# Where TensorE's two operands start in a partition: every pair of the second mixture 64 bytes apart modulo 512, and all tiles on multiples of 64 bytes

## The chip, the cores and the metric

One core of one Trainium2 chip runs the whole program in one launch. The metric is device time in microseconds (us), the median of several executions; lower is better. A core has five engines with queues of their own: TensorE (PE; its weight loads are listed apart as PEld), VectorE (DVE), ScalarE (ACT), GpSimd (POOL) and SyncE (SP, which only issues DMAs here). Tiles stand in SBUF, a memory of 128 partitions; a tile takes the same bytes of every partition, and "address" means here the byte at which it starts in each partition.

## The reference, cut to what matters

Three parts follow one another. The second mixture, to which the change belongs, takes most of the time.

```python
x = attention(q, k, v, M_prev, z_prev, beta)      # 2304 rows of 512
x = soft_mixture(x, phi, w1, w2)                   # 32 slots, 8 experts
# second mixture, N=2304 rows, D=512, E=8 experts, F=1024
P = exp(x @ w_gate - max)
for _ in range(8):
    P /= P.sum(1, keepdims=True) + 1e-09
    P /= P.sum(0, keepdims=True) + 1e-09
    P *= N / E
for e in range(E):
    h = np.maximum(x @ w1[e], 0.0)
    out += P[:, e:e+1] * (h @ w2[e])
```

## The kernel before, in words

The kernel first does the attention (to about 273 us), then the soft mixture (to about 327 us), then the second mixture. In the second mixture the work is cut into 72 units: 8 experts `e` by 9 groups `u` of 256 rows. Each unit is one `layer1` (8 matmuls of 256 columns, line 1035, which gives `x @ w1[e]` for 256 rows) and the product with `w2[e]`.

For the first six units (`RAW = 6`) the second product is made plainly, by `plain` (line 1321), with matmuls of 512 columns. For the other 66 it is made from seven half-size products in the manner of Strassen, in the order `ORDER = ("p5", "p1", "p7", "p6", "p2", "p3", "p4")`. A product (`product`, lines 1344 to 1357) is twelve matmuls of 256 columns: four steps `f`, and in each step three matmuls, since both factors are split into a high and a low part:

```python
for f in range(KH):
    nc.tensor.matmul(o_, hh[:, f, :], wh[:, f, :], start=f == 0, stop=False)
    nc.tensor.matmul(o_, hh[:, f, :], wl[:, f, :], start=False, stop=False)
    nc.tensor.matmul(o_, hl[:, f, :], wh[:, f, :], start=False, stop=f == KH - 1)
```

The first operand (`hh`, `hl`: tiles `a11`, `a12`, `a22`, `s1` to `s4`, each with `h` or `l` behind its name) is the stationary one, which a weight load (PEld) brings into the array: 128 numbers, 512 bytes, per partition. The second (`wh`, `wl`: tiles `T1`, `T2`, `T4`, and `BB1`, `BB2`, which hold the other quarters of `w2`) is the moving one: 256 numbers, 1024 bytes. In a row of the profile `y<-BB1h,s3h` the moving operand stands first and the stationary one second. `layer1` has `a4` (named `a` in the rows) as its stationary and `c4T` as its moving operand. The step `f` moves an operand on by 512, 1024 or 2048 bytes, so that it changes no address modulo 512.

The order of the work on TensorE, VectorE, ScalarE and GpSimd is written out by hand. TensorE goes through unit `g` as p5, p1, `layer1` of unit `g + 1`, p7, p6, p2, p3, p4, with some small matmuls put between (in four of an expert's nine units four transposes, line 1221, stand between p7 and p6; in one, `prepare_a`, line 992). The results of `layer1` are turned into the fourteen stationary tiles by VectorE, ScalarE and GpSimd (`hidden`, lines 1055 to 1076), and `collect` (line 1370) adds the products into `accA`, `accB` and `accD` on VectorE. `layer1` of the next unit may start once VectorE has written `a22l` (line 1072), which is the last to read its two PSUM buffers.

Tiles belong to pools, and pools stand one behind the other from the front of a partition; each tile takes its size rounded up to a multiple of 32 bytes. `T1` and `T2` of even experts and `BB1` are in pool `mA`, the stationary tiles in `mB`, `T4`, `T1` and `T2` of odd experts and `BB2` in `mC`, `a4` in `mD`. `cst` is the pool at the front of the program, with the tile `sacc`.

Of the kernel before, what the change touches and what calls it, by code (L numbers as in the profile page):

```python
# [8 lines left out]
F32 = mybir.dt.float32  # L9
BF16 = mybir.dt.bfloat16  # L10
F32R = mybir.dt.float32r
# [10 lines left out]
def infini_attention_soft_moe_sinkhorn_moe(  # L22
# [18 lines left out]
    E = moe2_w1.shape[0]  # L41
    FF = moe2_w1.shape[1] * moe2_w1.shape[4]
    NS = moe_phi.shape[2]
    SPE = NS // E
    P = 128
# [8 lines left out]
    NTT = N // P  # L54
# [14 lines left out]
    cst = ctx.enter_context(tc.tile_pool(name="cst", bufs=1))  # L69
# [16 lines left out]
        nc.vector.tensor_add(stk, stk, ident[:, 32 * j : 32 * j + 32])  # L86
    soT = cst.tile([P, KD, NS], F32, name="soT")
    wg_sb = cst.tile([P, KD, E], F32, name="wg_sb")
    sacc = cst.tile([P, 1], F32, name="sacc")
    mrow = [cst.tile([1, NS], F32, name=f"mrow{b}") for b in range(B)]  # L90


# [668 lines left out]
    with bctx:  # L761
# [57 lines left out]
        for g in range(E // 4):  # L819
# [3 lines left out]
            for n in range(FF // 512):  # L823
# [3 lines left out]
                for c in range(KD):  # L827
                    for j in range(4):
                        e = SPE * (4 * g + j)
# [41 lines left out]

    mA = ctx.enter_context(tc.tile_pool(name="mA", bufs=1, reuse_waits="tile"))
    mB = ctx.enter_context(tc.tile_pool(name="mB", bufs=1, reuse_waits="tile"))
    mC = ctx.enter_context(tc.tile_pool(name="mC", bufs=1, reuse_waits="tile"))
    mD = ctx.enter_context(tc.tile_pool(name="mD", bufs=1, reuse_waits="tile"))
    ps_l = ctx.enter_context(tc.tile_pool(name="ps_l", bufs=1, space=PSUM, reuse_waits="tile"))
# [91 lines left out]
        )  # L968


    sel = mD.tile([P, 4, 160], F32R, name="sel")
    nc.vector.tensor_scalar(
        out=sel.rearrange("p j c -> p (j c)"), in0=ones[:, 0:1].to_broadcast([P, 640]),
# [2 lines left out]
    for r in (0, 2, 4):  # L976
# [1 line left out]
        nc.vector.tensor_copy(  # L978
            sel[:, :, 32 * r : 32 * r + 32], ident.rearrange("p (j s) -> p j s", j=4)
        )  # L980
    a2s, a4s, G = {}, {}, {}

    def aux(nm):
        return ps_a.tile([P, 512], F32, tag="a", name=nm)
# [13 lines left out]
    def split_a(e):  # L998
        pa = a2s[e]
        ahi = mB.tile([P, 256], F32R, tag="ahi", name="ahi")  # L1000
        nc.scalar.activation(out=ahi, in_=pa[:, 0:256], func=AF.Copy)
        alo = mB.tile([P, 256], F32R, tag="alo", name="alo")
        nc.vector.tensor_tensor(
            out=alo, in0=pa[:, 0:256], in1=ahi.bitcast(F32), op=ALU.subtract
        )
        a2s[e] = ahi, alo
        a4s[e] = mD.tile([P, FF], F32R, tag="a4", name="a4", bufs=2)

    def spread_a(e, n):

# [97 lines left out]

    soR = soT.rearrange("p c (o s) -> p c o s", o=1)
    Pr = mB.tile([P, NTT, E], F32, name="Pr")  # L1110
    Cw = mD.tile([P, NTT, NS], F32, name="Cw")

    gsel = mD.tile([P, E + NS], F32R, name="gsel")
    m1 = mD.tile([P, 1], F32, name="m1")
    m2 = mD.tile([1, 1], F32, name="m2")

    def gate_slots():
        soB = G["soB"] = mB.tile([P, KD, 4, NS], F32, tag="c4", name="soB")
# [51 lines left out]
        nc.scalar.activation(out=Pr, in_=Pr, func=AF.Exp, bias=m1)  # L1170

    def balance_rows():
        rr = mB.tile([P, NTT], F32, tag="rr", name="rr")
        nc.vector.tensor_reduce(out=rr, in_=Pr, op=ALU.add, axis=AX.X)
        nc.vector.tensor_scalar_add(rr, rr, 1e-9)
        nc.vector.reciprocal(rr, rr)
        nc.vector.tensor_tensor(
            out=Pr, in0=Pr, in1=rr.rearrange("p (t o) -> p t o", o=1).to_broadcast([P, NTT, E]),
            op=ALU.mult,
        )  # L1180
        cs = G["cs"] = mB.tile([P, E], F32, tag="cs", name="cs")
        nc.vector.tensor_reduce(
            out=cs, in_=Pr.rearrange("p t e -> p e t"), op=ALU.add, axis=AX.X
        )
# [56 lines left out]
    for n in range(8):  # L1241
        beside(9 + 3 * n, balance_rows)
        beside(10 + 3 * n, sum_columns)
        beside(11 + 3 * n, balance_columns)
# [43 lines left out]
    for e in range(1, E):  # L1288
        v = NU * (e - 1)
        for i in range(5):  # L1290
            c_steps(v + 6 + i, e, 2 * i, min(2 * i + 2, NU))
        at(v, 0, load_w1, e, e % 2)
        at(v + 3 * (e == 1), 4, load_raw, e)
        at(v + 1, 3, prepare_a, e)
        at(v + 1, 4, split_a, e)
        for n in range(2):
            at(v + 1, 5 + 2 * n, spread_a, e, n)
            at(v + 1, 6 + 2 * n, store_a, e, n)
        for i in range(2):
            for n, nm in enumerate(("T1", "T2", "T4")):  # L1300

                s = 29 + 4 * (3 * i + n) if e == 1 else 7 * (v + 2 + 3 * i + n) + 1
                beside(s, w_sum, e, nm, i, "P")
                beside(s + 2 - (e == 1), w_hi, e, nm, i)
                beside(s + 3 - (e == 1), w_lo, e, nm, i, "P")
            at(v + 6 + i, 2, w_sum, e, "T3", i, "P")
        for nm, k in (("B11", 2), ("T3", 4), ("B21", 6), ("B22", 8)):
            for i in range(2):
                at(v + 8, k + i, w_hi, e, nm, i)
                at(v + 8, k + i + (nm[0] == "B" and nm[1] == "2"), w_lo, e, nm, i, "D" if nm == "B22" and i else "P")  # L1310
# [99 lines left out]
    with tc.manual_schedule(engines={E_.PE, E_.DVE, E_.Activation, E_.Pool}):  # L1410
# [4 lines left out]
        prepare_a(0)  # L1415
        gate_slots()
        split_a(0)
        spread_a(0, 0)
        spread_a(0, 1)
# [105 lines left out]
```

## Time and profile before

| | |
|---|---|
| time, median of 3 runs | 1181.48 us |
| lowest and highest | 1179.54 and 1184.17 us |
| the profiled execution's own time | 1182.51 us |
| its span, first to last instruction | 1180.7 us |
| mean granted TensorE clock | 0.986 |
| TensorE busy | 1120.1 us, 95% |
| VectorE, ScalarE, GpSimd busy | 865.7, 656.3, 641.8 us |
| chain that ended last, by engine | PE 75%, DVE 11%, ACT 7%, DMA 3%, issue 2%, POOL 1% |

All terms of a sum are in the time of the profiled execution, whose span is 1.81 us shorter than its own time and whose own time is 1.03 us above the median. The start of a row in a timeline is in us from the span's start. A matmul of this program lasts about 280 ns by its row, but the next one starts long before it ends: what TensorE needs for one more matmul is the distance from start to start.

### The profile page before, as it was taken

How to read it: one execution, taken by the hardware profiler on the slowest of the kernel's cores; microseconds unless marked ns; L12 is line 12 of the kernel's file. 1: busy time of each engine (PE TensorE's matmuls, PEld its weight loads, DVE VectorE, ACT ScalarE, POOL GpSimd, SP SyncE). 2: the span in 40 equal slices, each digit the busy share in tenths (PEclk: the TensorE clock that was granted, in tenths of full speed). 3: DMA queues.
4: the chain of work that ended last, by engine and by line, in shares of the span. 5: the costliest groups of instructions: out<-in, count | busy, mean ns of one | idle time of the engine just before them, and what ended most of it. 6: DMA issues, size and time to landing. Idle time of an engine off the chain costs nothing.

```text
span 1180.7 us, 24363 instructions
## 1 busy us (share of the span) xinstructions
PE 1120.1 (95%) x9247; PEld 1018.6 (86%) x9247; DVE 865.7 (73%) x1891; ACT 656.3 (56%) x1422; POOL 641.8 (54%) x585
## 2 busy tenths in 40 slices
PE   6899999979799999999999999999999999999998
PEld 4677777764287888999999999999999999999998
DVE  6888888874337566677778767777876777788886
ACT  6788888741233487546545644654564465456342
POOL 5433323200323297577677767767776776686443
PEclk9999999998989999999999999999999999999999
DMA  6677686249702004002100400210040031000111
GB/s 158 192 200 226 197 245 178 74 187 376 309 6 71 1 2 143 1 2 82 62 2 1 143 2 1 92 53 1 1 143 1 2 108 37 2 1 19 42 50 54
DMA packets 37412, 102.32 MB, mean 87 GB/s; under 512 B 6448, under 2 KB 13232, under 8 KB 33200
## 3 DMA queue, kind: packets, MB, share of 16 engines
q1 hardware_dynamic: 36864, 100.69, 26.5%
q8 instruction: 73, 1.20, 0.4%
q14 instruction: 43, 0.35, 0.1%
q10 hardware_dynamic: 432, 0.09, 0.0%
HBM read 96.04 MB, written 4.72 MB: 85 GB/s over the span
## 4 chain that ended last, share of the span: by engine, by line
PE 75%; DVE 11%; ACT 7%; DMA 3%; issue 2%; POOL 1%; SPq 0%; ACTq 0%; DVEq 0%; POOLq 0%
PE y L1356 16%; PE y L1354 16%; PE y L1355 16%; PE l L1035 6%; PE y L1321 5%; PE po L436 3%; PE pt L399 2%; ACT sm L360 2%; DMA wm<-in_moe_w_dram 1%; PE pa L992 1%; DVE sm L356 1%; PE pc L1221 1%; PE ph L830 1%; DVE f L1059 1%; DMA raw<-in_moe_w_dram 1%
## 5 line engine op out<-in xcount | busy, mean ns | idle before, releaser
L1059 DVE SCALAR_TENSOR_TENSOR f<-l,f 128x512 f32<-128x512 f32 x264 | 181.4, 687 | 56.6 <-ACT a11h L1065 44.4
L1076 POOL TENSOR_TENSOR s1l<-f,s1h 128x512 fp32r<-128x512 f32 x66 | 88.4, 1340 | 170.0 <-ACT s1h L1065 165.9
L1370 DVE TENSOR_TENSOR accA<-accA,y 128x512 f32<-128x512 f32 (+1 forms) x129 | 86.6, 671 | 57.1 <-PE y L1356 51.6
L1065 ACT ACTIVATE a12h<-l 128x512 fp32r<-128x512 f32 x72 | 43.1, 598 | 121.6 <-DVE f L1059 121.6
L1076 POOL TENSOR_TENSOR s4l<-f,s4h 128x512 fp32r<-128x512 f32 x66 | 86.0, 1303 | 39.9 <-ACT s4h L1065 39.8
L1370 DVE TENSOR_TENSOR accB<-accB,y 128x512 f32<-128x512 f32 x129 | 88.3, 684 | 13.7 <-PE y L1356 2.3
L1035 PE MATMUL l<-c4T,a 128*128 128x256 f32 x576 | 82.7, 286 | 9.2 <-DVE a22l L1072 8.3
L1076 POOL TENSOR_TENSOR s2l<-f,s2h 128x512 fp32r<-128x512 f32 x66 | 85.9, 1301 | 0.8 <-ACT s2h L1065 0.8
L1076 POOL TENSOR_TENSOR s3l<-f,s3h 128x512 fp32r<-128x512 f32 x66 | 86.0, 1303 | 0.3 <-ACT s3h L1065 0.3
L1035 PEld LDWEIGHTS l<-c4T,a 128*128 128x128 f32 x576 | 75.0, 190 | 12.4 <-DVE a22l L1072 10.8
L360 ACT ACTIVATE sm<-sm,mn 128x128 f32<-128x128 f32 (+3 forms) x128 | 71.1, 556 | 19.5 <-DVE mn L356 17.9
L965 POOL TENSOR_TENSOR BB1l<-raw,BB1h 128x512 fp32r<-128x512 f32 x32 | 41.0, 1293 | 68.9 <-ACT BB1h L959 68.9
L1354 PE MATMUL y<-T2h,s2h 128*128 128x256 f32 x264 | 76.9, 291 | 0.0
L1354 PE MATMUL y<-BB2h,a12h 128*128 128x256 f32 x264 | 75.0, 284 | 0.0
L1355 PE MATMUL y<-BB2l,s4h 128*128 128x256 f32 x264 | 74.6, 283 | 0.1
L1354 PE MATMUL y<-BB1h,a11h 128*128 128x256 f32 x264 | 73.4, 278 | 1.3 <-DVE accB L1370 1.3
L1356 PE MATMUL y<-T4h,a22l 128*128 128x256 f32 x264 | 74.6, 283 | 0.0
L1356 PE MATMUL y<-BB2h,a12l 128*128 128x256 f32 x264 | 74.5, 282 | 0.0
L1356 PE MATMUL y<-BB2h,s4l 128*128 128x256 f32 x264 | 74.5, 282 | 0.0
L1354 PE MATMUL y<-BB2h,s4h 128*128 128x256 f32 x264 | 74.5, 282 | 0.0
L1354 PE MATMUL y<-T4h,a22h 128*128 128x256 f32 x264 | 74.3, 281 | 0.0
L1356 PE MATMUL y<-T1h,s1l 128*128 128x256 f32 x264 | 74.1, 281 | 0.0
(313 smaller groups left out, 4219.0 us busy)
## 6 DMA issues: line engine op xcount, KB each, us to landing
wm<-in_moe_w_dram SPq DMA_DIRECT2D x32, 1024.0 KB, 7.7
w<-in_moe_w_dram SPq DMA_DIRECT2D x32, 512.0 KB, 4.4
raw<-in_moe_w_dram SPq DMA_DIRECT2D x32, 512.0 KB, 4.1
qd<-in_q_dram SPq DMA_DIRECT2D x30, 288.0 KB, 4.2
kd<-in_k_dram SPq DMA_DIRECT2D x30, 288.0 KB, 4.5
qp<-in_q_dram SPq DMA_DIRECT2D x16, 288.0 KB, 3.4
vt<-in_v_dram SPq DMA_DIRECT2D x16, 256.0 KB, 2.7
out_dram<-accB SPq DMA_DIRECT2D x18, 128.0 KB, 1.8
```

Source lines behind the costliest of these rows:

```text
L360: nc.scalar.activation(out=sm[:, 0:n], in_=sm[:, 0:n], func=AF.Exp, scale=-1.0, bias=mnc, accum_out=X.sums[:, i, h : h + 1],)
L436: nc.tensor.matmul(po[64 * h : 64 * h + 64, c0:w], X.vt[:, j, h, :], rhs, start=(j == 0), stop=(j == n - 1),)
L965: eng(g).tensor_tensor(out=w_tile(e, nm, "l")[:, h], in0=full(e, nm, i), in1=w_tile(e, nm, "h")[:, h].bitcast(F32), op=ALU.subtract,)
L1035: nc.tensor.matmul(ph[:, f, :], a4s[e][:, P * (KH * j + f) : P * (KH * j + f) + P], c4T[:, UT * u : UT * u + UT], start=True, stop=True,)
L1059: nc.vector.scalar_tensor_tensor(out=f_tile(g, nm), in0=ph(g, src), scalar=0.0, in1=b, op0=ALU.max, op1=op)
L1065: nc.scalar.activation(out=h_tile(g, nm, "h"), in_=ph(g, nm) if a else FU[g, nm], func=AF.Relu if a else AF.Copy)
L1076: nc.gpsimd.tensor_tensor(out=lo, in0=FU[g, nm], in1=hi, op=ALU.subtract)
L1321: nc.tensor.matmul(Y[g, i], X[g, f"a{i}{j}", "hhl"[n]][:, f, :], BB[j, "hlh"[n]][:, f].rearrange("p a c -> p (a c)"), start=j == 1 and f = ...
L1354: nc.tensor.matmul(o_, hh[:, f, :], wh[:, f, :], start=f == 0, stop=False)
L1355: nc.tensor.matmul(o_, hh[:, f, :], wl[:, f, :], start=False, stop=False)
L1356: nc.tensor.matmul(o_, hl[:, f, :], wh[:, f, :], start=False, stop=f == KH - 1)
L1370: nc.vector.tensor_tensor(out=acc, in0=acc, in1=y, op=ALU.add)
```

## The change

The place of tiles in SBUF is changed, and nothing else. Four things do it. `sacc` takes 64 bytes in place of 32, which moves everything behind it by 32 bytes. A new pool `mS` between `mB` and `mC` takes the small tiles `gsel`, `m1`, `m2`, `rr` and `cs`, with an unused tile of 96 bytes ahead of them. An unused tile of 64 bytes stands at the front of `mD`. `a4` and `Cw` are made before `sel`.

```diff
-    sacc = cst.tile([P, 1], F32, name="sacc")
+    sacc = cst.tile([P, 16], F32, name="sacc")[:, 0:1]
...
     mB = ctx.enter_context(tc.tile_pool(name="mB", bufs=1, reuse_waits="tile"))
+
+
+    mS = ctx.enter_context(tc.tile_pool(name="mS", bufs=1, reuse_waits="tile"))
+    mS.tile([P, 24], F32, name="gap")
     mC = ctx.enter_context(tc.tile_pool(name="mC", bufs=1, reuse_waits="tile"))
...
+    mD.tile([P, 16], F32, name="gap")
+    a4s = {0: mD.tile([P, FF], F32R, tag="a4", name="a4", bufs=2)}
+    Cw = mD.tile([P, NTT, NS], F32, name="Cw")
     sel = mD.tile([P, 4, 160], F32R, name="sel")
...
-    a2s, a4s, G = {}, {}, {}
+    a2s, G = {}, {}
...
-    a4s[e] = mD.tile([P, FF], F32R, tag="a4", name="a4", bufs=2)
+        if e:
+            a4s[e] = mD.tile([P, FF], F32R, tag="a4", name="a4", bufs=2)
...
-    Cw = mD.tile([P, NTT, NS], F32, name="Cw")
-
-    gsel = mD.tile([P, E + NS], F32R, name="gsel")
-    m1 = mD.tile([P, 1], F32, name="m1")
-    m2 = mD.tile([1, 1], F32, name="m2")
+    gsel = mS.tile([P, E + NS], F32R, name="gsel")
+    m1 = mS.tile([P, 1], F32, name="m1")
+    m2 = mS.tile([1, 1], F32, name="m2")
...
-        rr = mB.tile([P, NTT], F32, tag="rr", name="rr")
+        rr = mS.tile([P, NTT], F32, tag="rr", name="rr")
...
-        cs = G["cs"] = mB.tile([P, E], F32, tag="cs", name="cs")
+        cs = G["cs"] = mS.tile([P, E], F32, tag="cs", name="cs")
```

Addresses in the built programs, modulo 512 bytes:

| operand | before | after |
|---|---|---|
| stationary `a11`, `a12`, `a22`, `s3` | 480 | 0 |
| stationary `s1`, `s2`, `s4` | 96 | 0 |
| stationary `a4` (layer1) | 64 | 0 |
| moving `BB1`, `T1` and `T2` of even experts, `c4T` | 416 | 448 |
| moving `BB2`, `T4`, `T1` and `T2` of odd experts | 96 | 448 |

From these the distance, stationary address less moving address modulo 512, is:

| matmuls | moving, stationary | before | after |
|---|---|---|---|
| p1, p7 | BB1, a11 and BB1, s3 | 64 | 64 |
| p5, p6, even expert | T1, s1 and T2, s2 | 192 | 64 |
| p5, p6, odd expert | T1, s1 and T2, s2 | 0 | 64 |
| p3 | BB2, s4 | 0 | 64 |
| p2, p4 | BB2, a12 and T4, a22 | 384 | 64 |
| layer1 | c4T, a4 | 160 | 64 |
| plain, first half and second half | BB1 and BB2, with a11 to a22 | 64 and 384 | 64 |

On every engine the same instructions stand in the same order before and after. Of the waits that the built programs hold, six at the start of the second mixture or in it name another event, because a tile there now lies over another tile of an earlier stage; all the others are the same. In the attention most tiles move from 32 above a multiple of 64 to a multiple of 64, and a few of the large ones (`qp`, `x`, `qe`, `xT`) the other way.

## Rows read from the trace of the kernel before

**Rows 1.** The page, its first part: busy time of each engine.

```profile
PE 1120.1 (95%) x9247; PEld 1018.6 (86%) x9247; DVE 865.7 (73%) x1891; ACT 656.3 (56%) x1422; POOL 641.8 (54%) x585
```

**Rows 2.** Stretches of the second mixture: length, busy per engine, clock, DMA share, GB/s.

```profile
475.00:1084.00 609.00, 609.00 (x5268) 602.77 (x5269) 464.09 (x765) 328.27 (x619) 434.71 (x341) 1.00 0.11 36
1084.00:1180.70 96.70, 87.45 (x723) 85.62 (x721) 75.52 (x121) 34.71 (x62) 37.18 (x30) 1.00 0.15 49
```

**Rows 3.** Timeline, TensorE, a unit of expert 1: first matmul of each product.

```profile
495.88 1.12 PE L1035 MATMUL l<-c4T,a 128*128 128x256 f32 x8
496.83 0.28 PE L1354 MATMUL y<-BB1h,s3h 128*128 128x256 f32 x1
...
498.21 0.28 PE L1354 MATMUL y<-T2h,s2h 128*128 128x256 f32 x1
...
499.65 0.28 PE L1354 MATMUL y<-BB2h,a12h 128*128 128x256 f32 x1
...
501.08 0.28 PE L1354 MATMUL y<-BB2h,s4h 128*128 128x256 f32 x1
...
502.51 0.28 PE L1354 MATMUL y<-T4h,a22h 128*128 128x256 f32 x1
...
503.93 0.28 PE L1354 MATMUL y<-T1h,s1h 128*128 128x256 f32 x1
...
505.36 0.28 PE L1354 MATMUL y<-BB1h,a11h 128*128 128x256 f32 x1
...
506.75 0.52 PE L1035 MATMUL l<-c4T,a 128*128 128x256 f32 x3
```

**Rows 4.** The same of a unit of expert 2; p3 and p4 left out.

```profile
610.16 0.28 PE L1354 MATMUL y<-BB1h,s3h 128*128 128x256 f32 x1
...
611.55 0.28 PE L1354 MATMUL y<-T2h,s2h 128*128 128x256 f32 x1
...
612.91 0.28 PE L1354 MATMUL y<-BB2h,a12h 128*128 128x256 f32 x1
...
617.20 0.28 PE L1354 MATMUL y<-T1h,s1h 128*128 128x256 f32 x1
...
618.61 0.28 PE L1354 MATMUL y<-BB1h,a11h 128*128 128x256 f32 x1
...
619.98 0.76 PE L1035 MATMUL l<-c4T,a 128*128 128x256 f32 x5
```

**Rows 5.** Timeline, TensorE, a plain unit: 12 matmuls on BB2, 7 on BB1, transposes.

```profile
400.31 0.39 PE L1321 MATMUL y<-BB2h,a22h 128*128 128x512 f32 x1
...
403.10 0.39 PE L1321 MATMUL y<-BB1h,a11h 128*128 128x512 f32 x1
...
404.73 0.60 PE L1221 MATMUL pc<-ident,c 128*128 128x128 f32 x4
```

**Rows 6.** Instructions by line and form, 330 us to the end: ScalarE, mean ns.

```profile
L1055 ACT ACTIVATE f<-l 128x512 f32<-128x512 f32 x66 | 39.1, 592 | 62.5 <-PE l L1035 62.5
...
L62 ACT ACTIVATE a<-p 128x512 fp32r<-128x512 f32 x14 | 8.3, 594 | 10.0 <-PE p L1018 10.0
```

**Rows 7.** Timeline, VectorE, the unit of rows 4: start, length, idle before.

```profile
617.99 0.69 DVE L1072 SCALAR_TENSOR_TENSOR a22l<-l,a22h 128x512 fp32r<-128x512 f32 x1 [0.17 <-ACT a22h L1065]
```

**Rows 8.** Timeline, VectorE, last unit of expert 1 but one.

```profile
564.93 1.49 DVE L1059 SCALAR_TENSOR_TENSOR f<-l,f 128x512 f32<-128x512 f32 x2 [0.42 <-ACT a11h L1065]
...
572.67 0.69 DVE L1072 SCALAR_TENSOR_TENSOR a22l<-l,a22h 128x512 fp32r<-128x512 f32 x1 [0.40 <-ACT a22h L1065]
```

**Rows 9.** Timeline, TensorE: the layer1 that follows rows 8.

```profile
573.61 0.64 PE L1035 MATMUL l<-c4T,a 128*128 128x256 f32 x4
```

**Rows 10.** Waits of TensorE, 327 to 475 us: total us, times, longest.

```profile
PE l L1035 <- DVE a22l L1072: 4.6, 4, 1.7
```

**Rows 11.** Waits of all engines, 1000 us to the end: total us, times, longest.

```profile
PE l L1035 <- DVE a22l L1072: 3.7, 7, 0.6
```

**Rows 12.** Timeline, VectorE, a unit of the last expert.

```profile
1117.23 0.69 DVE L1370 TENSOR_TENSOR accA<-accA,y 128x512 f32<-128x512 f32 x1 [0.50 <-PE y L1356]
```

## The prediction

> **What bounds the kernel now.** I read the page first: TensorE is busy 95% of the span, far ahead of VectorE's 73% [rows 1]. Then the stretches, because a share over the whole program mixes stages. From 475 to 1084 us TensorE is busy 609.00 of 609.00 us, at full granted clock, while VectorE has 464, ScalarE 328 and GpSimd 435 us [rows 2]: half the program in which nothing else sets the time. In the last expert TensorE has 87.45 of 96.70 us [rows 2], so something else is felt there. Then the timeline of TensorE in single units, because a matmul's own length says nothing here: the time is the step from one start to the next, and the question is whether that step depends on the operands' addresses.
>
> It does. In a unit of expert 1 the starts of the products [rows 3] give: layer1 0.95 us, p7 1.38, p6 1.44, p2 1.43, p3 1.43, p4 1.42, p5 1.43, p1 1.39, together 10.87. Each product is twelve matmuls of 256 columns, so 1.43 is 119 ns for one and 1.38 is 115. The two short ones, p7 and p1, are those whose operands stand 64 bytes apart modulo 512; p3, p5 and p6 stand 0 apart, p2 and p4 384. Expert 2 is the control [rows 4]: p6 takes 1.36 there and p5 1.41, p7 and p1 1.39 and 1.37, and p2 to p4 together 4.29, as before (4.28). With 0.95 for layer1 the unit takes 10.77. p6 is the same line, the same shape and the same neighbours in both experts; only T2 lies elsewhere, 192 bytes from its partner and not 0. Nothing but a place in memory makes 1.44 into 1.36.
>
> **The change part by part.** The order of every engine stays, so each term is a step times a count.
>
> *The seven products.* After the change all of them have the distance that p1 and p7 have now. What does a whole product at 64 cost? The rows give 1.37 to 1.39, but both products begin behind matmuls with another distance (p1 behind p5, p7 behind layer1, 160 bytes). p6 of expert 2, which comes directly behind p7, takes 1.36, 113 ns each, the shortest that there is. I choose 1.365, between 1.36 and the better p1, since after the change no product has a neighbour of another distance except the small matmuls. Ends: 1.36 and p7's 1.385.
>
> *layer1* goes from 160 to 64. No row has it at 64; its matmuls have 256 columns too, so at the products' step it is 8/12 of 1.365, 0.91. Ends: 0.907, and 0.95 as now.
>
> *A unit* is then 7 x 1.365 + 0.91 = 10.465 us: 0.405 less in an odd expert, 0.305 less in an even one. Of the 72 units 52 lie in the stretch of rows 2, 25 of odd and 27 of even experts: 25 x 0.405 + 27 x 0.305 = 18.4 us.
>
> *What VectorE takes back.* layer1 of the next unit needs a22l. In the unit of rows 4 that is written by 618.68 [rows 7] and layer1 starts at 619.98: 1.30 us to spare, and a unit shorter by 0.4 leaves most of it. In the last unit but one of an expert VectorE has more to do: f starts at 564.93, a22l ends at 573.36, 8.43 us with 0.40 idle [rows 8], and layer1 starts at 573.61 [rows 9], 0.25 later. There 0.155 or 0.055 of the gain becomes a wait for a22l, queued behind VectorE's own work: six times, 0.6 us in all. Left: 17.8.
>
> *Before the stretch* TensorE waits for a22l already, 4.6 us in 4 waits [rows 10]. I count 0.1 us for each of five units (between nothing and 0.4), 0.5, and 0.04 for layer1 in each of six plain units, 0.2. The plain products gain nothing: twelve matmuls of 512 columns take 2.79 us on BB2 at 384 bytes, 232.5 ns each, and seven on BB1 at 64 take 1.63, 233 each [rows 5].
>
> *The last expert* waits for a22l in 7 units, up to 0.6 us [rows 11]. VectorE's chain there begins when p2 ends: it was idle 0.50 us for it [rows 12]. So what lies ahead of that counts (layer1 0.04, p7 0.015, p6 0.075, p2 0.065, together 0.195), and what is gained in p3, p4, p5 and p1 only makes the wait longer. Eight units give 1.6, and 0.2 more comes behind the last wait: 1.8.
>
> *Everything else that is moved* I take as nothing. For ScalarE a row shows it: 128x512 out of PSUM takes 594 ns into `a`, which lies on a multiple of 64 now, and 592 into f, which lies 32 above one [rows 6]. GpSimd and DMA have no such pair; their cover in the stretch is 174 us of idle GpSimd and a DMA share of 0.11 [rows 2], and without it each would cost or give what its instructions change, which I leave at zero, plus or minus 1 us for the attention. The waits that name another event name one of an earlier stage, over by then. `sacc`'s step over 64 bytes is used at a few instructions of one column.
>
> **Sum.** 17.8 + 0.5 + 0.2 + 1.8 = 20.3. The span becomes 1160.4, the execution's own time 1162.2, and against the median, 1.03 lower, 1161.2 us, 1.7% faster.
>
> [...]
>
> **The rivals.**
>
> *The head of a product stays.* If the short step has to be found anew in every product, as p7 seems to, each costs 1.385 and layer1 its 0.95: a unit of 10.645, 0.225 and 0.125 less. 25 x 0.225 + 27 x 0.125 = 9.0, with about 1.2 from the rest, gives 1171.3 us. For it: p7 is no faster than 1.38 in either unit. Against: p6 of expert 2 has no dear head. VectorE as the bound in all units, as in the last expert, would end near the same time (52 x 0.195 = 10.1), but 1.30 us of slack speaks against that. Chance 0.12 together.
>
> *No difference.* The steps differ for another reason than the distance (what other engines read at that time, say), and the change keeps each at its step: 1181.5 us. For it: p5 gains only 0.02 between the experts, while p6 gains 0.08 for the same move. Against: other engines do the same in both. Chance 0.06.
>
> *The place counts, not the distance.* No row has an operand at 0 or at 448. If a stationary operand at a multiple of 512 makes the two reads collide whatever the distance, every product runs at 1.43 and layer1 at 0.95: a unit of 10.96, 0.09 and 0.19 more. 25 x 0.09 + 27 x 0.19 = 7.4, and about 0.8 in the last expert, give 1189.7 us, slower. It decides where a product at the new places takes more than 1.40, the mean of the seven now. For it: p6 and p5 share both addresses in each expert and still differ, so distance alone is not the whole rule. Against: p1 and p7 are short in both experts with unlike neighbours. Chance 0.08.
>
> **How the numbers follow.** The forecast has 0.74. Its own ends: with 1.36 and 0.907 a unit is 10.427, 25 x 0.443 + 27 x 0.343 = 20.3, with nothing taken back, 2.0 before the stretch and 3.2 in the last expert, 25.5 in all: 1156.0; the other end meets the first rival at 1171.3. With 1 us for the unknown engines the range is 1155 to 1172, which leaves out the last two rivals and little else. A measurement of this kernel can tell about 0.5%, 5.9 us, from no change: faster 0.86, same 0.06, slower 0.08.
>
> **What the profile of the changed kernel would show.** Right: the starts of all seven products 1.36 to 1.37 us apart, odd and even experts alike, layer1 0.91, a unit without transposes near 10.47; TensorE still busy throughout the long stretch; waits for a22l in six more units and longer in the last expert. p6 of odd experts shows it best: from 1.44. Wrong: products of 1.385 with a dear head (first rival), steps as now with odd and even experts unlike (second), p1 and p7 longer than 1.39 (third). The prediction fails too if a22l is waited for in most units, or if VectorE's or GpSimd's own instructions change their length.

## The result, and the profile after

Before 1181.63 us (1179.54 to 1184.17, 4 runs), after 1166.58 us (1165.04 to 1171.02, 4 runs): 0.988 of the time, with an interval of 0.985 to 0.991. The run of after that was profiled took 1166.2 us, with a span of 1164.4 us. Lines 1035, 1072, 1221, 1255, 1354 to 1356 and 1370 of before are 1043, 1080, 1228, 1262, 1361 to 1363 and 1377 now.

The first part of the page of after, which answers to [rows 1]:

```profile
PE 1104.8 (95%) x9247; PEld 999.5 (86%) x9247; DVE 871.8 (75%) x1891; ACT 658.4 (57%) x1422; POOL 643.4 (55%) x585
```

The same instructions, with 15.3 us less of TensorE's time. The stretches of [rows 2] in after:

```profile
475.00:1084.00 609.00, 606.32 (x5344) 598.62 (x5343) 483.92 (x784) 335.18 (x631) 440.18 (x345) 1.00 0.11 37
1084.00:1164.40 80.40, 73.17 (x612) 70.95 (x612) 63.41 (x99) 28.15 (x48) 30.80 (x25) 1.00 0.15 49
```

In the same 609 us there are 76 matmuls more. All but 0.3 of TensorE's 2.68 us of idle time are the last expert's, which begins at 1058.58 now, inside the stretch. The granted clock is 1.00 as before, so it is no clock that moved the time.

The timeline of TensorE in after, a unit of expert 1, each product's first matmul; beside [rows 3]:

```profile
493.12 1.07 PE L1043 MATMUL l<-c4T,a 128*128 128x256 f32 x8
494.03 0.28 PE L1361 MATMUL y<-BB1h,s3h 128*128 128x256 f32 x1
...
495.39 0.28 PE L1361 MATMUL y<-T2h,s2h 128*128 128x256 f32 x1
...
496.75 0.28 PE L1361 MATMUL y<-BB2h,a12h 128*128 128x256 f32 x1
...
498.11 0.28 PE L1361 MATMUL y<-BB2h,s4h 128*128 128x256 f32 x1
...
499.47 0.28 PE L1361 MATMUL y<-T4h,a22h 128*128 128x256 f32 x1
...
500.83 0.28 PE L1361 MATMUL y<-T1h,s1h 128*128 128x256 f32 x1
...
502.19 0.28 PE L1361 MATMUL y<-BB1h,a11h 128*128 128x256 f32 x1
...
503.55 0.50 PE L1043 MATMUL l<-c4T,a 128*128 128x256 f32 x3
```

Seven products of 1.36 us, a layer1 of 0.91, a unit of 10.43: 92 matmuls, 113.3 ns from start to start. Expert 2's units without transposes are 10.43 too; the difference between odd and even experts is gone.

The units with transposes tell another story. Two neighbours in expert 2, timeline of TensorE in after (p7 stands ahead of the transposes, p6 right behind them):

```profile
646.84 1.10 PE L1043 MATMUL l<-c4T,a 128*128 128x256 f32 x8
647.78 0.28 PE L1361 MATMUL y<-BB1h,s3h 128*128 128x256 f32 x1
...
649.19 0.60 PE L1228 MATMUL pc<-ident,c 128*128 128x128 f32 x4
649.55 0.37 PE L1361 MATMUL y<-T2h,s2h 128*128 128x256 f32 x1
...
651.01 0.28 PE L1361 MATMUL y<-BB2h,a12h 128*128 128x256 f32 x1
...
652.37 0.28 PE L1361 MATMUL y<-BB2h,s4h 128*128 128x256 f32 x1
...
657.81 1.07 PE L1043 MATMUL l<-c4T,a 128*128 128x256 f32 x8
658.71 0.28 PE L1361 MATMUL y<-BB1h,s3h 128*128 128x256 f32 x1
...
660.08 0.60 PE L1228 MATMUL pc<-ident,c 128*128 128x128 f32 x4
660.43 0.36 PE L1361 MATMUL y<-T2h,s2h 128*128 128x256 f32 x1
...
661.93 0.28 PE L1361 MATMUL y<-BB2h,a12h 128*128 128x256 f32 x1
...
663.34 0.28 PE L1361 MATMUL y<-BB2h,s4h 128*128 128x256 f32 x1
...
669.17 1.19 PE L1043 MATMUL l<-c4T,a 128*128 128x256 f32 x8
```

p7 takes 1.41 us ahead of the first transposes (647.78 to 649.19); behind them p2 takes 1.36 (651.01 to 652.37), and so does all that follows, through layer1 and the next p7, 1.37. Behind the next transposes p2 takes 1.41 again (661.93 to 663.34), and the rest of that unit is long too. p6 pays for the break itself, with 1.46 or 1.50 us. So with equal operands and equal distances there are two steps, 113.3 and 117.7 ns, which I call the short and the long one. TensorE keeps the one it has for a unit on end and changes only at a break in the row of equal matmuls: the transposes, `prepare_a`, a wait. By the starts of layer1 these units take 10.88 to 11.41 us; in before they took 11.25 to 11.31. In 10 of the 23 of them the products behind the transposes have the long step; the longest, at 11.36 and more, have a wait besides, read from the starts further down.

Where the time came from, by the starts of layer1 in both timelines. In before these four bound the stretches:

```profile
327.14 2.08 PE L1035 MATMUL l<-c4T,a 128*128 128x256 f32 x8 [0.79 <-DVE a L66]
...
470.59 0.86 PE L1035 MATMUL l<-c4T,a 128*128 128x256 f32 x5
...
1074.40 1.12 PE L1035 MATMUL l<-c4T,a 128*128 128x256 f32 x8
...
1158.20 1.23 PE L1035 MATMUL l<-c4T,a 128*128 128x256 f32 x8 [0.49 <-DVE a22l L1072]
```

In after the same four:

```profile
325.29 2.08 PE L1043 MATMUL l<-c4T,a 128*128 128x256 f32 x8 [0.85 <-DVE a L66]
...
468.45 1.19 PE L1043 MATMUL l<-c4T,a 128*128 128x256 f32 x8 [0.29 <-DVE a22l L1080]
...
1058.58 1.07 PE L1043 MATMUL l<-c4T,a 128*128 128x256 f32 x8
...
1142.66 1.19 PE L1043 MATMUL l<-c4T,a 128*128 128x256 f32 x8 [0.56 <-DVE a22l L1080]
```

| stretch | before, us | after, us | gained | forecast |
|---|---|---|---|---|
| to the first layer1 | 327.14 | 325.29 | 1.85 | 0 |
| first units, to 470.59 / 468.45 | 143.45 | 143.16 | 0.29 | 0.7 |
| 53 units, to 1074.40 / 1058.58 | 603.81 | 590.13 | 13.68 | 17.8 |
| last expert, up to its last layer1 | 83.80 | 84.08 | -0.28 | 1.8, with the next row |
| from there to the end | 22.50 | 21.74 | 0.76 | |
| span | 1180.7 | 1164.4 | 16.3 | 20.3 |

Of the 13.68 us, 24 units without transposes gave 9.36 (12 went from 10.87 and 12 from 10.77 to 10.43), 23 units with transposes 3.55 (from 11.28 to 11.12 on the mean), and the six units with `prepare_a` 0.78.

### The profile page after: what moved, and what is told of

Read it like the earlier page. It is cut to its first block, busy times and chain, and to the rows that moved or that the text cites. A ratio compares the mean times of both kernels' runs of the same rounds, so it can differ in the third digit from the quotient of the medians.

```text
span 1164.4 us, 24365 instructions
## 1 busy us (share of the span) xinstructions
PE 1104.8 (95%) x9247; PEld 999.5 (86%) x9247; DVE 871.8 (75%) x1891; ACT 658.4 (57%) x1422; POOL 643.4 (55%) x585
## 4 chain that ended last, share of the span: by engine, by line
PE 76%; DVE 12%; ACT 7%; issue 2%; POOL 1%; DMA 1%; SPq 0%; ACTq 0%; DVEq 0%; POOLq 0%
PE y L1361 16%; PE y L1362 16%; PE y L1363 16%; PE l L1043 6%; PE y L1328 5%; PE po L436 3%; PE ph L830 2%; ACT sm L360 2%; PE pt L399 2%; PE pso L848 1%; PE pa L999 1%; PE pc L1228 1%; DVE sm L356 1%; DVE f L1067 1%; DVE accB L1262 1%
## 5 line engine op out<-in xcount | busy, mean ns | idle before, releaser
L1043 PEld LDWEIGHTS l<-c4T,a 128*128 128x128 f32 x576 | 72.4, 190 | 14.5 <-DVE a22l L1080 12.8
L1362 PE MATMUL y<-T2l,s2h 128*128 128x256 f32 x264 | 73.4, 278 | 0.0
L1363 PE MATMUL y<-BB1h,s3l 128*128 128x256 f32 x264 | 73.2, 277 | 0.2 <-POOL s3l L1084 0.2
L1363 PE MATMUL y<-T2h,s2l 128*128 128x256 f32 x264 | 73.3, 278 | 0.0
L1361 PE MATMUL y<-T1h,s1h 128*128 128x256 f32 x264 | 73.3, 278 | 0.0
```

The costliest lines, as they stand in the source:

```text
L1043: nc.tensor.matmul(ph[:, f, :], a4s[e][:, P * (KH * j + f) : P * (KH * j + f) + P], c4T[:, UT * u : UT * u + UT], start=True, stop=True,)
```

## The experiments

The theory after the result: the step depends on the distance between the two operands, as predicted; what is missing lies in the long step and in the last expert. Rivals: that the multiples of 64 do it, not the distance; that more distance would do more; that the transposes' own operands hold the long step. A letter that stands for a theory in an expectation holds for that expectation alone. "Before" is run beside each.

**The shift alone**, in the kernel before. It puts every tile 32 bytes on and leaves each distance as it was.

```diff
-    sacc = cst.tile([P, 1], F32, name="sacc")
+    sacc = cst.tile([P, 16], F32, name="sacc")[:, 0:1]
```

> The kernel before with one line changed: sacc takes 64 bytes, so that all tiles move by 32 bytes and stand on multiples of 64, with the distances of TensorE's operands as before. Theory (the distance between stationary and moving operand modulo 512 sets the step): a unit of an odd expert stays at 10.87 us, of an even one at 10.77, the median at 1181 to 1183 us. Rival (multiples of 64 bytes matter to some engine by themselves): the time moves towards the changed kernel's 1166.6, or VectorE's, ScalarE's or GpSimd's mean durations change.

1182.53 us against 1182.28, ratio 1.000 (0.998 to 1.002). Units of 10.87 and 10.77 as in before. Multiples of 64 by themselves give nothing.

**The distance alone**: the changed kernel without the shift, stationary operands at 480 and moving ones at 416.

```diff
-    sacc = cst.tile([P, 16], F32, name="sacc")[:, 0:1]
+    sacc = cst.tile([P, 1], F32, name="sacc")
```

> The changed kernel with sacc at 4 bytes again: every pair of operands 64 bytes apart, but all of them 32 bytes above a multiple of 64 (stationary at 480, moving at 416). Theory: units without transposes take 10.43 us in all experts as in the changed kernel, median 1164 to 1169 us. Rival (the place on multiples of 64 or at the start of a 512-byte row counts): units above 10.5 us and a median above 1172.

1168.85 us, ratio 0.988 (0.984 to 0.991): the whole gain, within the intervals. Its profile shows the two steps expert by expert. The last unit without transposes in expert 1 and in expert 2, timeline of TensorE:

```profile
516.08 1.07 PE L1043 MATMUL l<-c4T,a 128*128 128x256 f32 x8
...
526.51 0.73 PE L1043 MATMUL l<-c4T,a 128*128 128x256 f32 x5
...
617.30 1.10 PE L1043 MATMUL l<-c4T,a 128*128 128x256 f32 x8
...
628.13 1.11 PE L1043 MATMUL l<-c4T,a 128*128 128x256 f32 x8
```

10.43 us in expert 1 and 10.83 in expert 2, which is 117.7 ns for each of 92. Experts 1, 3 and 6 have the one, 2, 4 and 5 the other, each from its `prepare_a` on. So the median came as expected, but not 10.43 in all experts. The profile is of the longest of the four runs, 1172.92 us.

**The transposes' operand moved**: `ident`, which the transposes read, goes to 448, 64 bytes from its partner, as all other pairs are.

```diff
+    stk = cst.tile([P, NS], F32, name="stk")
+    wg_sb = cst.tile([P, KD, E], F32, name="wg_sb")
+    sacc = cst.tile([P, 16], F32, name="sacc")[:, 0:1]
...
-    stk = cst.tile([P, NS], F32, name="stk")
-    wg_sb = cst.tile([P, KD, E], F32, name="wg_sb")
-    sacc = cst.tile([P, 16], F32, name="sacc")[:, 0:1]
```

> The changed kernel with ident moved to 448 modulo 512 by making three small tiles ahead of it, so that the transposes' operands (ident moving, c4 stationary) are 64 bytes apart too instead of 384. Theory A (a transpose throws the next products into the slow step of 117.7 ns because its own operands have another distance): units with transposes all take 10.87 to 10.97 us, none 11.1 to 11.4, median near 1160. Theory B (the break itself does it, whatever the distance): units with transposes as in the changed kernel, some at 11.1 to 11.4 us, median within 3 us of 1166.6.

1170.86 us, ratio 0.991 (0.987 to 0.994), and both steps are there: odd experts have 10.83 and 11.27 throughout, even ones 10.43 and then 10.88 to 11.43. It is not the transposes' distance, and theory A, that it is, fell. Theory B had the units right, but its time, within 3 us of 1166.6, was missed by 1.3. The profile is of the longest of six runs (1165.33 to 1177.35).

**All products at distance 0.** The small tiles stand ahead of the stationary ones in `mB` here and in the six runs on other distances, in such a choice that the stationary ones come to another address, and their lines in `mS` go; the moving ones stay at 448.

```diff
-    mS.tile([P, 24], F32, name="gap")
...
+        mB.tile([P, 24], F32, name="gap")
+        gsel = mB.tile([P, E + NS], F32R, name="gsel")
+        SM["rr"] = mB.tile([P, NTT], F32, name="rr")
+        m1 = mB.tile([P, 1], F32, name="m1")
+        m2 = mB.tile([1, 1], F32, name="m2")
+        SM["cs"] = mB.tile([P, E], F32, name="cs")
```

> The changed kernel with the small tiles put ahead of the products' stationary tiles, so that these stand at 448 modulo 512, at the same address as the moving ones (distance 0); layer1 keeps 64. Theory: the products step at 119 to 120 ns as p3 did before, 1.43 us each, odd and even experts alike, a unit without transposes 10.9 us, and the time is 1185 to 1192 us. Rival (place counts, not distance): 448 is a good place for both and units stay near 10.43.

1190.98 us in one run, slower than each of the 15 of before (up to 1186.26). Timeline of TensorE, four products of a unit of expert 2:

```profile
605.61 0.28 PE L1358 MATMUL y<-BB2h,s4h 128*128 128x256 f32 x1
...
607.05 0.28 PE L1358 MATMUL y<-T4h,a22h 128*128 128x256 f32 x1
...
611.37 1.11 PE L1043 MATMUL l<-c4T,a 128*128 128x256 f32 x8
```

Each takes 1.44 us, 120 ns for a matmul, and units are 11.02 (11.44 with transposes) in every expert: no second step. Against the short step at 64, every product costs 0.08 us more at 0.

**Other distances.** 128, 256, 448 (64 with the other sign) and 96, each by other tiles ahead of the stationary ones:

```diff
 distance 128
+        m1 = mB.tile([P, 1], F32, name="m1")
+        m2 = mB.tile([1, 1], F32, name="m2")
 distance 256
+        mB.tile([P, 24], F32, name="gap")
+        SM["rr"] = mB.tile([P, NTT], F32, name="rr")
 distance 448
+        mB.tile([P, 24], F32, name="gap")
+        gsel = mB.tile([P, E + NS], F32R, name="gsel")
+        SM["rr"] = mB.tile([P, NTT], F32, name="rr")
+        m1 = mB.tile([P, 1], F32, name="m1")
 distance 96
+        m1 = mB.tile([P, 1], F32, name="m1")
```

> The changed kernel with the products' operands 128 bytes apart modulo 512 (stationary at 64, moving at 448); layer1 keeps 64. Theory A (64 is one point of a curve; further from 0 is as good or better, up to the middle): products of 1.36 us and perhaps no second state, a unit without transposes 10.43 us or near it, time 1160 to 1168. Theory B (two reads at any distance but 64 meet again, as at 384 and 160 before): products of 1.41 to 1.44 us, unit 10.8 to 11.0, time 1180 to 1190.

> The same at 256 bytes (stationary at 192), the middle of the 512. Theory A: 1.36 us and one state only, since the two reads are as far apart as they can be, 1158 to 1165. Theory B: 1.41 to 1.44 us, 1180 to 1190.

> The same at 448 bytes, which is 64 the other way round (stationary at 384, behind the moving operand instead of ahead of it). If only the size of the distance counts, units of 10.43 and 10.84 us as in the changed kernel, 1164 to 1172. If the sign counts (the stationary read must run ahead of the moving one), products of 1.41 to 1.44 us, 1178 to 1191.

> The same at 96 bytes (stationary at 32). If the two states at 64 (113.3 and 117.7 ns a matmul) come of a distance that is just short of enough, 96 has the fast one alone: units of 10.43 and 10.87 us, 1158 to 1163. If they come of a phase that the break sets, both states appear again, 1163 to 1172.

One run each, before 1182.48: 1184.93, 1189.07, 1172.50 and 1185.96 us. Products of 1.42 to 1.43 at 128, 1.44 at 256, 1.36 at 448 (behind `prepare_a`; 1.41 behind most transposes), 1.44 at 96 in most units without transposes, and 1.41 in two of them and behind most transposes. So farther isn't better, the sign doesn't matter, and 96 isn't good for being more than 64. At 448 the time is 0.5 us above the range that was expected, and at 96 neither expectation came true: both had the short step. At 448 the step changes where nothing was expected to change it: layer1, which keeps its 64, runs at 113 ns behind products of 1.41, and the p7 behind it takes 1.36. What was left was a period of 128, that is, that only the remainder counts when the distance is divided by 128. It was put to the test with **192 and 320**, which are 64 more than 128 and 256:

```diff
 distance 192
+        mB.tile([P, 24], F32, name="gap")
+        m1 = mB.tile([P, 1], F32, name="m1")
 distance 320
+        mB.tile([P, 24], F32, name="gap")
+        gsel = mB.tile([P, E + NS], F32R, name="gsel")
```

> The changed kernel with the products' operands 192 bytes apart (stationary at 128). So far 64 and 448 gave the two states of 113.3 and 117.7 ns, and 0, 96, 128 and 256 gave 118 to 120. Theory (what counts is the distance modulo 128: 64 is good, 0 is bad): both states again, units without transposes at 10.43 or 10.84 us, time 1164 to 1174. Rival (only 64 to either side is good): 10.9 to 11.0 us and 1183 to 1190.

> The same at 320 bytes (stationary at 256), which is 64 modulo 128 too. Theory: as at 192. Rival: 10.9 to 11.0 us.

1174.05 and 1171.51 us, before 1183.62: both quicker than before, both with units of 10.43, and both with the long step in many units behind a break.

In these runs the moving operands stay at 448, so the stationary address alone could be what counts. The two runs that split the change answer that: in the shift alone both operands of p3 stand at 128, and it takes 1.43 us; in the distance alone the stationary ones stand at 480, which is 96 modulo 128, and the short step is there.

| distance | modulo 128 | product, us | time, us (runs) |
|---|---|---|---|
| 0 | 0 | 1.44 | 1190.98 (1) |
| 256 | 0 | 1.44 | 1189.07 (1) |
| 128 | 0 | 1.42 to 1.43 | 1184.93 (1) |
| 96 | 96 | 1.41 or 1.44 | 1185.96 (1) |
| 64, changed kernel | 64 | 1.36 or 1.41 | 1166.58 (4), 1169.61 (6) |
| 192 | 64 | 1.36 or 1.41 | 1174.05 (1) |
| 320 | 64 | 1.36 or 1.41 | 1171.51 (1) |
| 448 | 64 | 1.36 or 1.41 | 1172.50 (1) |

**No transposes**: are they the break that changes the step? Experts 1 to 7 work here without their turned copies of `c` and compute with expert 0's.

```diff
-        at(v, 2, turn_c, e, u0, u1)
-        at(v, 3, store_c, e, u0, u1)
```

> The changed kernel without the transposes of the weights c of experts 1 to 7 and without the copies that store them, so that these experts compute with expert 0's c: the four transposes between p7 and p6 in 33 units fall out. Theory (a break in the row of equal matmuls sets the state, and it holds until the next break): all units of an expert behind prepare_a take the same time, 10.43 or 10.84 us each, with no change inside an expert. Rival (the state wanders by itself, or another engine's access sets it): units of one expert differ as before, between 10.43 and 11.0.

1171.39 us, before 1183.62. No unit changes its step inside an expert: in each of the six whole experts the first seven units behind `prepare_a` take 10.83 or 10.84. That fits the theory. What I had not expected is which step it was: the long one, behind every `prepare_a`, where the changed kernel has the short one. Without transposes the kernel is therefore no faster than with them.

**The changed kernel again**, five rounds, with no edit.

> The changed kernel itself, once more and with more rounds. Theory (which state follows a break is left to small differences in time): the profile shows another pattern of units at 10.43, 10.84, 10.88 and 11.2 to 11.4 us than the first one, its single times spread over some 1164 to 1178 us, wider than those of the kernel before, and the ratio to before is 0.985 to 0.991. Rival (the pattern is fixed by the program): the same units are slow as in the first profile, and the times spread no more than before's.

1169.61 us (1166.83 to 1172.88, 6 runs) against 1183.62 (1179.88 to 1186.55, 11 runs), ratio 0.989 (0.987 to 0.991). Units of 10.43 behind each `prepare_a` again; behind the transposes the two steps come in another order than in the first profile (four units of expert 2: 10.89, 11.07, 11.19, 11.11, where the first had 10.88, 11.41, 10.97, 11.36). So it isn't fixed by the program alone. The times spread no wider than before's, though they had been expected to.

None of these versions was faster than the changed kernel.

## Why the prediction was right, and where its sum was not

**The distance sets the step: right.** The chosen 1.365 us for a product and 0.91 for layer1 came out as 1.36 and 0.91, the unit as 10.43 (forecast 10.465), odd and even experts alike. The two runs that split the change show that it is the distance and no address by itself, and distance 0 in all products that it works both ways. A product takes 1.36 us at 64, with the short step, and 1.44 at 0. That the reads of the two operands collide or meet, as the third rival and theory B of distance 128 put it, was the author's guess: no row shows a read.

**The units with transposes: the mis-sized term.** The step that failed is "0.405 less in an odd expert, 0.305 less in an even one" for all 52 units. It was taken for granted that a distance of 64 has one step. It has two, and the long one is worth 92 x 4.4 ns = 0.40 us a unit, as much as the whole gain. The 24 units behind `prepare_a` gave 0.39 each; the 23 with transposes gave 0.15. With 0.39 each they would have given 9.0 and not 3.55, and the 53 units some 19. Of the 5.4 us that are missing, by the lengths of all products of these units, some 3.7 are the long step and 1.7 are waits for VectorE.

**Waits for a22l in six more units: right, but too small.** VectorE's chain was to take back 0.6 us. The stretch has five such units and not six, and in all five layer1 did wait. The view of waits has only one of them between 475 and 1070 us, 0.2 us long: a row of TensorE lasts 0.28 us and the next starts 0.11 behind it, so a wait shorter than the difference leaves no idle time between rows. The starts show it. Ahead of the layer1 at 669.17 above, in after:

```profile
668.43 0.69 DVE L1080 SCALAR_TENSOR_TENSOR a22l<-l,a22h 128x512 fp32r<-128x512 f32 x1 [0.40 <-ACT a22h L1073]
...
668.91 0.28 PE L1363 MATMUL y<-BB1h,a11l 128*128 128x256 f32 x1
```

a22l is written by 669.12; layer1 starts 0.05 later, and 0.26 behind the last matmul of p1. In before the same layer1 started 0.33 after a22l. The five waits are 0.15 to 0.33 us, 0.95 in all, and a layer1 behind one takes 1.02 to 1.04 us and not 0.91, another 0.6: 1.5 us where the sum had 0.6. Before 475 the wait grew from 4.6 [rows 10] to 5.2:

```profile
PE l L1043 <- DVE a22l L1080: 5.2, 5, 1.8
```

A second wait was not in the sum. In four experts the second group of transposes waits for `c`, which VectorE writes: p7 takes 1.55 us there, 0.76 in all. Expert 2, VectorE in before, then GpSimd, VectorE and TensorE in after:

```profile
641.43 0.71 DVE L1206 TENSOR_TENSOR cP<-Cw,Pr 128x128 f32<-128x128 f32 x1
...
634.85 1.31 POOL L960 TENSOR_TENSOR ft<-raw,ft 128x512 f32<-128x512 f32 x1
634.88 1.43 DVE L1213 TENSOR_TENSOR cP<-Cw,Pr 128x128 f32<-128x128 f32 x1
...
636.75 1.00 DVE L1223 TENSOR_TENSOR c<-cP,chi 128x256 f32<-128x256 f32 x1 [0.44 <-ACT chi L1218]
...
637.89 0.63 PE L1228 MATMUL pc<-ident,c 128*128 128x128 f32 x4
```

`c` is written by 637.75. The `cP` ahead of it takes twice its time. It starts right behind GpSimd's `ft` now, where in before `ft` was more than half done (640.69 to 641.98); the `cP` of the next group, at 646.23 with no GpSimd instruction beside it, takes 0.28. So one of the prediction's own signs of being wrong did show: VectorE's instructions changed their length. From 475 to 1084 us the mean of the 24 128x128 `cP` went from 0.52 to 0.80 us, and VectorE is busy for 6.1 us more in the whole program.

**The last expert: the step that failed is "VectorE's chain there begins when p2 ends".** p2 did end earlier. Timeline of VectorE and GpSimd in a unit of the last expert, in before beside [rows 12]:

```profile
1117.66 1.30 POOL L1076 TENSOR_TENSOR s3l<-f,s3h 128x512 fp32r<-128x512 f32 x1
...
1117.95 1.54 DVE L1255 TENSOR_TENSOR accB<-accB,accA 128x512 f32<-128x512 f32 x1
...
1119.42 0.41 DVE L1258 TENSOR_TENSOR accD<-accD,accA 128x256 f32<-128x256 f32 x1
```

In after, with the add at the very end of the program as its last row:

```profile
1113.08 0.69 DVE L1377 TENSOR_TENSOR accA<-accA,y 128x512 f32<-128x512 f32 x1 [0.28 <-PE y L1363]
...
1113.72 1.31 POOL L1084 TENSOR_TENSOR s3l<-f,s3h 128x512 fp32r<-128x512 f32 x1
1113.80 1.77 DVE L1262 TENSOR_TENSOR accB<-accB,accA 128x512 f32<-128x512 f32 x1
...
1115.50 0.41 DVE L1265 TENSOR_TENSOR accD<-accD,accA 128x256 f32<-128x256 f32 x1
...
1158.74 0.69 DVE L1262 TENSOR_TENSOR accB<-accB,accA 128x512 f32<-128x512 f32 x1
```

And in the kernel with distance 0:

```profile
1126.94 1.28 POOL L1084 TENSOR_TENSOR s3l<-f,s3h 128x512 fp32r<-128x512 f32 x1
...
1127.24 1.53 DVE L1259 TENSOR_TENSOR accB<-accB,accA 128x512 f32<-128x512 f32 x1
1128.69 0.41 DVE L1262 TENSOR_TENSOR accD<-accD,accA 128x256 f32<-128x256 f32 x1
```

VectorE's wait for p2 shrank from 0.50 to 0.28, and the add behind it grew from 1.54 to 1.77, as in the five units from 1102 to 1150 us: the 0.22 us are gone again. With no GpSimd instruction beside it the same add takes 0.69. In all three kernels the next VectorE instruction starts 0.46 to 0.48 us after `s3l` ends, whenever the add began behind the start of `s3l`. Once in after the add was the first to start, at 1078.91, by 0.04 us: it took 0.69, and `s3l` 1.80. So the three traces have 0.69 us for the add alone and 1.52 to 1.78 behind the start of `s3l`; what makes it longer there, no row shows. By these starts the chain runs from layer1 over ScalarE and VectorE's f to GpSimd's s1l, s2l and s3l, then to the add and a22l, and TensorE's products are not in it; a unit of the last expert takes 11.61 to 11.64 us in the changed kernel and in the kernel with distance 0 alike, from the third on, though their products differ by 0.08. It was not tried with GpSimd's work moved away. Only the work behind the last layer1 gained, 0.76.

**The first 327 us: not forecast, not explained.** The 1.85 us there are within what runs differ by: the first layer1 starts between 325.29 and 328.48 in the profiles of all kernels, 327.14 in before. Without them the kernel gained 14.5 us of the 20.3, and the median's 15 us are in line with that.

**The rivals.** "The head of a product stays": no product has a head; 494.03 to 495.39 is 1.36 like the rest. A dear start is seen only behind a break: p6 behind the transposes (1.46 to 1.50), layer1 behind a wait (1.02 to 1.04). Its time, 1171.3, is near the measured 1166.58, but the long step and the waits took what is missing, not the head. The line of 1.40 us that the third rival draws as the mean of the seven products is 1.42 in an odd expert and 1.40 in an even one; nothing hangs on it. "No difference" and "the place counts" fell with the two runs that split the change.

**What stays open**: what decides at a break which step follows, and why the period, by the eight distances of the table, is 128 bytes. It is not the whole rule, since a product takes 1.42 to 1.43 us at 128 and 1.44 at 0 and 256. Distances of 32 modulo 128 were not tried in the products (layer1 of before, at 160, took 0.95 for eight, 119 ns).

## What to carry to other kernels

Where TensorE is busy throughout and each matmul brings its own weights, look at the step from start to start, and at the two operands' addresses: here a distance of 64 modulo 128 was worth 6% of a product against 0 at the short step and 2% at the long one (1.36 and 1.41 us against 1.44). Price every kind of unit by its own rows; the step behind a break need not be the one that you measured in mid-row. Read waits of TensorE from the starts of its rows too: five of 0.15 to 0.33 us showed as one of 0.2. And when VectorE waits for TensorE by the profile, look whether the instruction behind the wait takes longer beside one of GpSimd (here 1.52 to 1.78 us against 0.69 by itself): then the wait can be slack, and shortening it from 0.50 to 0.28 us gave nothing here.

## What the runs showed of the hardware that was not expected

- A row of equal matmuls (256 columns, each with a weight load, clock 1.00) runs at one of two steps, 113.3 or 117.7 ns, when the distance is 64, 192, 320 or 448. In the changed kernel, with 64 everywhere, it keeps it for 92 matmuls and more, across tiles and layer1, and changes at breaks alone; with 192 or 448 in the products and 64 in layer1 it went from the long to the short step at layer1 too.
- At distance 0 and 256 the step is 120 ns, at 128 118.5, at 96 117.3 or 120.
- An add of two SBUF tiles on VectorE, 0.69 us by itself, took 1.52 to 1.78 when it started behind GpSimd's 1.3 us subtract, and the next VectorE instruction started 0.46 to 0.48 us behind the subtract's end. Where the add started 0.04 us ahead of the subtract, it took 0.69 and the subtract 1.80. The chain of work that ended last puts the longer add down as VectorE's own time (`accB` L1262, 10.8% of it from 1084 us on), not as a wait.
